# An earlier function table load, small idle products and a new opening order in a memory attention and feed-forward kernel

## The chip, the cores and the metric

The kernel runs on one core of a Trainium2 chip. The time is the device time of one execution in microseconds; of several executions the median counts. A core has the engines TensorE (PE in the profile, its weight loads PEld), VectorE (DVE), ScalarE (ACT), GpSimd (POOL), and queues that issue DMA transfers, here those of SyncE (SP) and ScalarE.

## What is computed

Attention in which the keys and values of a sequence of 576 are first summed into 32 memory slots per head, and a two-layer feed-forward network behind it:

```python
def _attn_ref(q, k, v, phi):                    # 8 batches, 8 heads, 576 rows, head size 64
    a = phi - np.max(phi, axis=2, keepdims=True)
    a = np.exp(a)
    a = a / (np.sum(a, axis=2, keepdims=True) + 1e-09)
    k_m = np.einsum('bhsm,bhsd->bhmd', a, k)
    v_m = np.einsum('bhsm,bhsd->bhmd', a, v)
    scores = scale * np.matmul(q, k_m.transpose(0, 1, 3, 2))
    scores = scores - np.max(scores, axis=-1, keepdims=True)
    attn = np.exp(scores)
    attn = attn / (np.sum(attn, axis=-1, keepdims=True) + 1e-09)
    return np.matmul(attn, v_m).astype(np.float32)

def _moe_ref(x, w_in, w_out):                   # 4608 rows, 512 -> 2048 -> 512
    h = x @ w_in
    g = np.maximum(0.01 * h, h)
    return (g @ w_out).astype(np.float32)
```

The weights arrive as 64-bit floats, and the kernel turns their bits into 32-bit floats itself.

## The kernel before

The kernel is written as small steps, each a Python function under a short name in the table `steps`. Three strings list the names in the order in which the steps are issued: OPENING (line 39), LATER (line 70), and both are run once, one after the other, under a manual schedule (line 1609). Each engine works through its own instructions in that order, and so does each DMA queue; semaphores make an engine wait where it needs another's result. The order is thus written out by hand, and a step stands behind all earlier steps that use its engine.

Names that matter here. `a0.` to `a7.` are the batches' attention, `i0.` to `i3.` and `o0.` to `o3.` the quarters of w_in and w_out, `u0.` to `u7.` the first group of rows (192 rows of each of two blocks) by eighths of the hidden width, `P8`, `V8` and so on the groups behind it, `z.` products that compute nothing that is used.

For batch 0:

- `a0.phi0` to `phi3` load phi by pairs of heads, two of them on ScalarE's queue (`load_phi`, line 542); `k0`.., `v0`.. and `q0`.. load the rest on SP's queue.
- `A10` to `A13` (line 622) take maxima over the rows on VectorE, `A2` (663) transposes them, `A3` (667) makes two diagonal matrices of the maxima, one on VectorE and one on ScalarE (673), and `B0` (679) spreads them to all partitions by products with ones.
- `B10` to `B12` (688) subtract the maximum, `B20` to `B22` (694) are the exponentials on ScalarE, `B30` to `B32` (710 to 719) add them up.
- `C100` to `C102` (738) are the slot sums over k and `C11` those over v: 72 f32 products each of 64 rows by 32 columns, four column places and two row places of TensorE's array. `C2`, `C30`, `C3k`, `C31` divide by the sums.
- `R0` to `R5` (933) transpose q, `Q0` to `Q5` keep it; `D10`, `D3` make the keys' transpose, `D11`, `D5` the values'.
- `E10` to `E13` (979) are the scores, `E20` to `E23` (1030) flip them, and `S01` to `S06` are the first chunk's softmax (maximum, subtraction, exponential on ScalarE at 1065, sum, division, flip).
- `a0.T` (566) is one exponential of a column of ones; its output is overwritten later. ScalarE's first activation makes the compiler put a table load ahead of it on that engine.

For the weights, each quarter comes in three pieces of 768, 768 and 512 columns: `ld` loads one on SP's queue (w_in pieces as several transfers, 381 and 385), `h` and `y` turn the low and the high words (395 and 406 on ScalarE, or 397 on VectorE for `h`), `t` puts them together on VectorE (415). The pieces lie in eight slots in turn, which the parts of q use too, so a load waits until the slot's last reader is done. `b` are the squares' sums for a bound (420).

`f00.1` (1156) folds the values of batch 0 into a quarter of w_in, and `f00.2` (1521) copies the result on ScalarE. `u0.P0` (1248) is a product of the first group with it, `V` the leaky function (1255), `O` the down projection (1335): sixteen halves of six f32 products' passes each. `ci.`, `co.`, `e.` and `e2.` make the scales for the later f16 products.

The idle products of `z.f` are one f32 product of 128 by 128 by 512, those of `z.2` two bf16 products of this size, all into one accumulator that nobody reads (1544).

Of the kernel before, what the change touches and what calls it, by code (L numbers as in the profile page):

```python
# [49 lines left out]
i2.h2 o0.t2 i2.h0 u2.V0 o1.t0 a0.S17 o1.t1 o1.ld2 o2.ld0 i2.y0 i2.y1 o2.ld1 u1.O1 u3.P1 u3.V1 o1.h2  # L50
a0.D4 i2.t0 a1.phi a1.kv0 o2.y0 o1.y2 i2.h1 o2.y1 o2.h1 i2.t1 u2.O0 i2.t2 a1.A1 o1.t2 f02.1 u2.P1
u3.P0 a1.A2 o2.ld2 a1.kv1 o2.h0 u2.V1 f02.2 u3.V0 u4.P0 a1.A3 a1.B0 i2.b o2.h2 o2.t0 a1.kv3 a1.kv2
a1.q1 u3.O0 o2.y2 u4.P1 a1.B10 o2.t1 a1.B20 a1.C10 i1.b o2.t2 a1.B3 u4.V0 o1.b a1.C2 a1.q0 a1.C30
u4.V1 a1.C31 a1.C3k o2.b i3.ld0 a1.C4 a1.Q1 u2.O1 a1.Q0 a0.S18 i3.ld1 a1.D11 a1.D2 a1.D10 a1.D4
a1.D5 a1.D3 u3.O1 i3.h1 i3.ld2 o3.ld2 i3.y0 i3.h0 a1.E1 o0.b i3.y1 o3.ld0 i3.h2 i3.y2 a1.E21 i3.t0
# [131 lines left out]
def kernel(  # L187
# [1349 lines left out]
    def idle_products(n, f32):  # L1537
        if not idle_sums:
            idle_sums.append(ps_o.tile([P, NF, P], F32, name="po"))
# [3 lines left out]
        for _ in range(n):  # L1543
            nc.tensor.matmul(idle_sums[0], by, of, start=True, stop=True)  # L1544
# [97 lines left out]
```

## Time and profile before

| | us |
|---|---|
| median of 3 runs | 653.37 |
| lowest and highest of them | 652.44, 655.95 |
| the profiled execution | 652.1 |
| its span, first to last instruction | 650.0 |

What the profile shows of TensorE in the opening, by stretches of 10 us: busy time with the number of products, and the DMA share:

| from, to us | TensorE busy, products | DMA share |
|---|---|---|
| 0 to 10 | 7.69, 19 | 0.84 |
| 10 to 20 | 9.75, 231 | 1.00 |
| 20 to 30 | 7.71, 210 | 0.86 |
| 30 to 40 | 9.99, 42 | 0.97 |
| 40 to 50 | 10.00, 33 | 1.00 |

In the profile, times are microseconds from the first instruction. A line number names the line of the kernel that issued an instruction; a row of a timeline has its start, its duration, the engine, the line, the operation, what is written from what, the count, and in brackets the idle time ahead of it with what ended that. "issue" is time in which an engine waited for nothing that the profile shows. A row of the chain of waits has a start, a length, and what the end of the kernel waited for at that time.

### The profile page before, as it was taken

How to read it: one execution, taken by the hardware profiler on the slowest of the kernel's cores; microseconds unless marked ns; L12 is line 12 of the kernel's file. 1: busy time of each engine (PE TensorE's matmuls, PEld its weight loads, DVE VectorE, ACT ScalarE, POOL GpSimd, SP SyncE). 2: the span in 40 equal slices, each digit the busy share in tenths (PEclk: the TensorE clock that was granted, in tenths of full speed). 3: DMA queues.
4: the chain of work that ended last, by engine and by line, in shares of the span. 5: the costliest groups of instructions: out<-in, count | busy, mean ns of one | idle time of the engine just before them, and what ended most of it. 6: DMA issues, size and time to landing. Idle time of an engine off the chain costs nothing.

```text
span 650.0 us, 17218 instructions
## 1 busy us (share of the span) xinstructions
PE 636.9 (98%) x7305; PEld 482.5 (74%) x7305; DVE 511.0 (79%) x856; ACT 394.2 (61%) x682; POOL 29.9 (5%) x41
## 2 busy tenths in 40 slices
...
GB/s 302 342 363 288 321 42 123 10 23 89 195 9 33 133 151 69 125 100 42 31 126 136 3 32 43 20 126 147 33 22 79 22 29 20 16 29 7 33 1 50
DMA packets 85885, 61.17 MB, mean 94 GB/s; under 512 B 62128, under 2 KB 69040, under 8 KB 85808
## 3 DMA queue, kind: packets, MB, share of 16 engines
...
q8 instruction: 57, 0.93, 0.6%
q10 hardware_dynamic: 480, 0.43, 0.2%
q14 instruction: 20, 0.16, 0.1%
...
## 4 chain that ended last, share of the span: by engine, by line
PE 90%; DMA 5%; ACT 3%; DVE 2%; issue 1%; SPq 0%; ACTq 0%; DVEq 0%
PE po L1446 31%; PE ph L1378 22%; PE po L1335 13%; PE ph L1248 7%; PE ph L1446 5%; PE pa L1156 4%; PE pa L738 3%; PE po L1481 1%; DMA arena<-in_phi_dram 1%; DMA arena<-in_moe_w_out_dram 1%; PE pa L963 1%; PE po L1544 1%; DMA arena<-in_moe_w_in_dram 1%; DMA arena<-in_q_dram 1%; ACT wi L1394 1%
## 5 line engine op out<-in xcount | busy, mean ns | idle before, releaser
L1446 PEld LDWEIGHTS <-arena 128*128 128x128 f16 x2184 | 209.7, 98 | 32.6 <-issue 9.5
L1394 ACT ACTIVATE wi<-ph,g_sc 128x256 f32<-128x256 f32 (+1 forms) x224 | 99.0, 464 | 166.2 <-PE ph L1378 160.4
L1378 PE MATMUL ph<-a,w_mem 128*128 128x256 f16 (+3 forms) x1440 | 145.3, 246 | 2.9 <-ACT wi L1394 2.9
L1378 PEld LDWEIGHTS <-w_mem 128*128 128x128 f16 x1440 | 114.6, 98 | 17.0 <-issue 6.3
L1446 PE MATMUL po<-wo,arena 128*128 128x256 f16 x936 | 122.2, 273 | 0.3 <-issue 0.3
L1446 PE MATMUL po<-arena 128*128 128x256 f16 x936 | 122.1, 273 | 0.0
L1335 PE MATMUL po<-wo,arena 128*128 128x512 f16 (+1 forms) x384 | 110.0, 433 | 0.0
L1423 DVE TENSOR_TENSOR arena<-arena 128x1024 f16<-128x1024 f32 x52 | 63.5, 1222 | 22.4 <-ACT arena L1419 22.4
L1423 DVE TENSOR_TENSOR arena<-wi,arena 128x768 f16<-128x768 f32 (+1 forms) x60 | 54.6, 911 | 10.1 <-ACT arena L1419 10.1
L1415 DVE TENSOR_TENSOR arena<-wi 128x256 f32<-128x256 f32 x104 | 40.4, 430 | 26.2 <-ACT wi L1394 25.7
L1419 ACT CAST arena<-arena 128x1024 f16<-128x1024 f32 x52 | 54.4, 1046 | 7.6 <-DVE arena L1415 7.3
L1248 PE MATMUL ph<-a,w_mem 128*128 128x192 f16 (+2 forms) x304 | 52.3, 317 | 0.0
L1335 PEld LDWEIGHTS <-arena 128*128 128x128 f16 x288 | 27.8, 98 | 29.8 <-issue 0.6
L1419 ACT CAST arena<-wi 128x768 f16<-128x768 f32 (+1 forms) x60 | 46.5, 776 | 1.6
L1415 DVE TENSOR_TENSOR arena<-wi,arena 128x256 f32<-128x256 f32 x104 | 45.7, 439 | 1.8
L1446 PE MATMUL ph<-wo,arena 128*128 128x256 f16 x312 | 42.6, 273 | 0.0
L1121 POOL TENSOR_TENSOR a<-t,a 128x128 f16<-128x128 f32 (+3 forms) x17 | 21.7, 1297 | 442.4 <-ACT a L1116 442.4
L1335 PEld LDWEIGHTS po<-wo,arena 128*128 128x128 f32 x96 | 17.8, 190 | 20.9 <-issue 17.9
L1156 PE MATMUL pa<-wi,vT 64*32 64x512 f16 (+1 forms) x704 | 29.4, 420 | 0.0
L1255 ACT ACTIVATE arena<-ph,g_sc 128x384 f32<-128x384 f32 x32 | 18.5, 580 | 15.8 <-PE ph L1248 15.5
L1248 PEld LDWEIGHTS <-w_mem 128*128 128x128 f16 x240 | 20.6, 98 | 9.7 <-issue 3.6
L1189 ACT ACTIVATE w_mem<-pa 128x512 f16<-128x512 f32 x40 | 22.7, 596 | 8.5 <-PE pa L1156 7.4
...
## 6 DMA issues: line engine op xcount, KB each, us to landing
...
arena<-in_moe_w_out_dram SPq DMA_DIRECT2D x8, 768.0 KB, 8.3
...
```

Of the source, the lines that this page charges most:

```text
L738: nc.tensor.matmul(var["pk"][g][hh * M:(hh + 1) * M, cs], ld["phi"][rows, hh, j, :], ld["kv", hh][rows, kinds[0]:kinds[-1] + 1, j, :], sta ...
L1121: nc.gpsimd.tensor_tensor(piece(lo, tb), piece(t2, tb), piece(hi, tb), ALU.subtract)
L1156: nc.tensor.matmul(pf[g][cols, :], lhs, rhs, start=(n == 0), stop=(n == len(passes) - 1), tile_position=(g * D, hh * M),)
L1189: nc.scalar.activation(tiles(halves(w16(b, j), g)[:, 0]), w(g), AF.Copy, scale=ws)
L1248: nc.tensor.matmul(ph[:, t0:t0 + n * SB], lhs, rhs, start=(m == 0), stop=(m == len(seq) - 1))
L1335: nc.tensor.matmul(po, lhs, rhs, start=(f == 0 and m == 0), stop=(f == NQ * NF - 1 and m == len(seq) - 1),)
L1378: nc.tensor.matmul(ph[:, t0:t0 + n], lhs, rhs, start=(m == 0), stop=(m == len(seq) - 1))
L1394: nc.scalar.activation(dst, ph, AF.Prelu, scale=g_sc2[:, j:j + 1], alpha=SLOPE)
L1415: nc.vector.tensor_tensor(gt[:, x], y, z, op)
L1419: nc.scalar.copy(dst[:, 0], src)
L1423: nc.vector.tensor_tensor(dst[:, 1], src, dst[:, 0], ALU.subtract)
L1446: nc.tensor.matmul(acc, g[:, x, s, u], rhs, start=(h == 0 and j == 0 and u == 0 and m == 0), stop=(j == NQ - 1 and u == 1 and m == 2), ski ...
```

## The change

The diff changes the two strings with the order and adds one kind of step.

- `a0.T` stands right behind the four loads of phi; before, it stood behind `A3` and `B0`.
- A new step `z.t` makes eight f32 products of 64 rows by 32 columns with 64 moving columns, on ones, in the four column places of the array in turn; it stands seven times at the head. The f32 idle products at the head are gone. In all the opening has seven `z.t`, three `z.2`, two `z.1` and four `z.f`, where it had ten `z.2` and six `z.f`.
- The rest of the opening has a new order: `i0.ld0` behind the last load of v, the largest part of phi (`B12`, `B22`) ahead of the others, `C11` ahead of `S02`, `o0.h0` ahead of `f00.2`, `o0.ld1` right behind `o0.ld0`, `u1.P0` ahead of `u0.P0`, `W11.p` and the loads of batch 2 earlier, `e2.` later, and more of this kind.
- From `P8.0` on LATER is the same but for the steps that have moved across the joint of the two strings.

```diff
 OPENING = """
-z.f z.f z.2 a0.phi1 a0.A11 a0.phi2 a0.phi0 a0.phi3 a0.A10 a0.A13 z.f a0.A12 a0.k1 a0.k2 a0.k0 a0.A2
-a0.k3 a0.q3 a0.q1 z.2 z.2 a0.A3 a0.B0 z.f a0.q0 a0.B10 a0.B11 a0.T a0.B20 a0.B21 a0.q2 z.2 a0.B12
-a0.C100 i0.ld1 a0.v3 a0.v1 a0.B22 a0.B30 a0.C101 a0.B31 i0.ld0 a0.C102 a0.R3 a0.B32 a0.C2 a0.Q3
-a0.C30 a0.C3k a0.R1 a0.v0 a0.Q1 a0.R0 a0.D10 a0.v2 a0.D3 a0.R2 a0.Q2 i0.y1 i0.h1 a0.Q0 a0.E10 a0.E11
-i0.ld2 a0.q4 z.2 z.2 z.2 z.2 z.f a0.E21 z.f a0.C11 a0.E20 a0.q5 a0.S01 i0.h0 a0.S02 i0.t1 a0.S03
-o0.ld0 i0.y0 a0.C31 z.2 z.2 i0.h2 i0.y2 a0.D11 a0.S04 i0.t0 a0.R5 a0.R4 a0.D5 i0.t2 a0.S05 i1.ld0
-o0.ld1 i1.ld2 a0.Q5 a0.Q4 a0.S06 f00.1 a0.E12 f00.2 i1.ld1 a0.E13 u0.P0 i0.b a0.C4 a0.E23 a0.E22
...
+a0.phi1 a0.phi2 a0.phi0 a0.phi3 a0.T z.t z.t z.t z.t z.t z.t z.t z.2 a0.A11 a0.A10 a0.A12 a0.A13 a0.A2
+a0.A3 z.1 a0.k3 a0.k0 a0.k1 a0.B0 a0.B12 a0.B10 a0.k2 z.2 a0.B22 a0.B11 z.2 a0.B20 a0.q3 a0.C100
+a0.q0 a0.B30 a0.q1 a0.B21 a0.C101 a0.q2 a0.B31 a0.B32 a0.C102 a0.C2 a0.R3 a0.v3 a0.v0 a0.v1 i0.ld1
+a0.Q3 a0.C30 a0.R1 a0.R0 a0.Q1 a0.v2 a0.C3k a0.D10 a0.Q0 a0.R2 a0.D3 a0.Q2 z.1 a0.E11 a0.E10 i0.ld0
+a0.E20 z.f i0.y1 i0.h1 a0.E21 i0.ld2 a0.q4 a0.S01 a0.C11 a0.S02 a0.q5 a0.C31 a0.S03 i0.h0 i0.y0 z.f
+z.f z.f i0.t1 a0.D11 a0.R5 i0.h2 i0.y2 o0.ld0 o0.ld1 a0.D5 a0.S04 i0.t0 i0.t2 a0.Q5 a0.R4 a0.Q4
+a0.S05 o0.h0 f00.1 a0.E12 i1.ld0 f00.2 a0.S06 i1.ld2 i1.ld1 i0.b a0.E13 u1.P0 u1.V0 o0.y0 u0.P0
...
-    def idle_products(n, f32):
+    def idle_tile():
         if not idle_sums:
             idle_sums.append(ps_o.tile([P, NF, P], F32, name="po"))
+        return idle_sums[0]
+
+    def idle_products(n, f32):
...
-            nc.tensor.matmul(idle_sums[0], by, of, start=True, stop=True)
+            nc.tensor.matmul(idle_tile(), by, of, start=True, stop=True)
...
+    def idle_tiles():
+        for x in range(8):
+            rows, cols = slice(0, 64), slice(x % 4 * 32, (x % 4 + 1) * 32)
+            nc.tensor.matmul(
+                idle_tile()[cols, 0, 0:64], ones[rows, cols], ones[rows, 0:64],
+                start=True, stop=True, tile_position=(0, x % 4 * 32),
+            )
+
+    steps["z.t"] = idle_tiles
```

More of the change, by code (lines that the diff above doesn't have):

```diff
@@ L50 @@
[L50 to L55, printed above, removed]
@@ new lines @@
+o0.ld2 i2.ld0 u0.V0 a0.C4 a0.E23 i1.h0 a0.D2 i1.y2 i1.h2 o0.y1 a0.E22 o1.ld0 o0.t0 o0.h1 a0.S11
+i1.t2 i1.y0 o0.t1 i1.t0 i1.h1 u1.P1 u0.P1 u0.V1 a0.S12 i2.ld2 i2.ld1 u1.V1 i1.y1 o0.y2 u0.O0 o0.h2
+i2.y0 i1.t1 o0.t2 o1.ld1 i2.h0 u1.O0 f01.1 o1.y0 a0.S13 i2.h2 f01.2 o1.ld2 i2.y1 u0.O1 u3.P0 i2.y2
+o2.ld1 a0.S14 o1.h0 o1.y1 i2.t0 i2.h1 a0.S15 o2.ld0 u3.V0 o1.h1 o2.h1 i2.t1 u2.P0 a1.phi i2.t2 u2.V0
+o1.t0 o2.ld2 o1.t1 a1.kv1 o1.h2 a1.kv0 f02.1 a1.kv2 u3.P1 u1.O1 o1.y2 u3.V1 f02.2 a1.A1 u2.O0 o1.t2
@@ new lines @@
+o2.h0 o2.y1 o2.h2 o2.y0 a1.A2 a1.A3 u4.P0 i2.b a0.D4 o2.t1 a1.B0 a1.B10 u2.P1 a1.B20 i1.b o2.y2
+u3.O0 a1.kv3 a1.q0 u2.V1 a0.S16 o2.t0 a1.q1 u4.V0 a1.C10 a1.B3 a1.C2 i3.ld1 u4.P1 o0.b a0.S17 u2.O1
+a1.C30 o2.t2 a1.C31 a1.C3k a1.C4 a1.Q0 a1.D11 u5.P0 a1.D10 a1.D2 o2.b i3.y1 u4.V1 a0.S18 i3.ld0
+i3.ld2 a1.D5 u5.V0 u3.O1 a1.D3 i3.y0 a1.Q1 i3.h1 a1.D4 i3.h0 i3.t1 i3.y2 a1.E1 o3.ld0 o3.ld2 o1.b
+i3.t0 a1.E20 o3.ld1 u4.O0 u5.P1 i3.h2 i3.t2 a1.E22 f03.1 i3.b o3.y2 o3.y0 o3.h0 f03.2 o3.h2 a1.E21
+ci.1 u5.O0 a1.S11 ci.2 a1.S01 a1.S12 a1.S02 a1.S03 w1.1 o3.y1 a1.S13 u5.V1 o3.t0 o3.t2 a1.S04 ci.3
@@ L61 @@
+o3.h1 u6.P0 u6.V0 ci.4 u4.O1 e. a1.S05 o0.s0 u7.P0 u7.P1 o3.t1 a2.kv0 w0.2 w1.2 o3.b W11.p co.1
+a1.S14 co.2 W01.h0 u7.V0 W01.l0 a2.phi a1.S06 u6.O0 u7.V1 i0.k1 a1.S07 W01.h1 co.3 u6.P1 a1.S15 co.4
+o0.s1 a2.A1 u7.O0 a1.S08 o0.k0 u6.V1
 """
@@ L76 @@
-o3.s3 V11.1 P12.0 o1.m1 O10.0 C11 V12.0 o1.n1 L11 P12.1 o1.s2 O10.1 o1.m2 W03.l1 o1.s3 V12.1 W03.l0
-a2.A3 o1.n2 o2.k0 C12 W13.p o2.k2 o2.l0 W13.h1 P13.0 W13.h0 W13.l1 P13.1 W13.l0 V13.0 o2.k1 L12
-V13.1 O11.0 o1.m3 P14.0 o2.l1 V14.0 C13 o2.s0 P14.1 L13 o2.m0 O11.1 a2.B10 V14.1 o1.n3 o2.n0 o2.s1
-P15.0 a2.B20 C14 o2.m1 O12.0 o2.s2 V15.0 o2.n1 o2.m2 a2.C10 L14 P15.1 o2.s3 a2.B3 O12.1 o2.l2 a2.q0
-V15.1 o2.n2 o3.s0 a2.q1 o3.k1 o3.k0 o3.l1 P16.0 P16.1 o3.k2 O13.0 V16.0 C15 o2.m3 o3.s1 O13.1 V16.1
```

44 lines of the change are left out of this document (21 added, 23 removed).

## The prediction

> **What bounds the kernel now.** First the page, for who is busy over the whole span.
>
> ```profile
> span 650.0 us, 17218 instructions
> PE 636.9 (98%) x7305; PEld 482.5 (74%) x7305; DVE 511.0 (79%) x856; ACT 394.2 (61%) x682; POOL 29.9 (5%) x41
> q8 instruction: 57, 0.93, 0.6%
> ```
>
> TensorE is busy for 98% of the span, so time can come only from stretches in which it works on nothing useful. The stage table (start and end, its length, busy time and count of TensorE products, of its weight loads, of VectorE, ScalarE and GpSimd, then granted clock, DMA share and GB/s) splits the span at the first product of the first group's up projection (28.4) and at the first f16 product of the second group (104.4).
>
> ```profile
> 0.00:21.25 21.25, 18.68 (x347) 9.69 (x347) 12.23 (x25) 9.48 (x16) 1.04 (x11) 1.00 0.93 325
> 21.25:23.31 2.06, 0.01 (x2) 0.01 (x1) 1.34 (x4) 0.00 (x0) 0.00 (x0) 1.00 1.01 400
> ...
> 28.40:104.40 76.00, 75.42 (x502) 35.56 (x503) 59.01 (x112) 65.61 (x102) 11.38 (x13) 1.00 0.69 239
> 104.40:650.00 545.60, 537.91 (x6378) 434.26 (x6374) 435.51 (x713) 315.26 (x556) 17.44 (x17) 1.00 0.26 62
> 139.10:141.30 2.20, 2.20 (x141) 1.99 (x144) 2.20 (x4) 0.28 (x1) 0.00 (x0) 1.00 0.00 0
> ...
> 0.00:28.40 28.40, 12.17 (x32) 4.49 (x32) 1.00 0.89 316
> ```
>
> The last row counts L1544, the idle products, alone: 12.17 us of the first 28.4. From 28.4 to 104.4 TensorE idles 0.6 us of 76. The 7.7 idle us of the third stage lie in code whose order the change leaves as it is. So the change is worth what it moves **the first L1248 product, at 28.36**, as far as nothing between there and 104.4 takes it back. The chain of work gives the path to it.
>
> ```profile
> 0.73 3.06 DMA wi<-in_phi_dram
> ...
> 8.32 0.41 ACT r1k L673
> 8.77 0.43 PE pa L679 x2
> ...
> 16.34 3.55 PE po L1544 x12
> 19.89 1.37 PE po L738 x88
> 21.25 2.06 issue
> 23.31 0.42 PE po L738 x22
> ...
> 25.68 1.15 PE pa L1156 x14
> ...
> 27.93 0.43 PE pa L979 x16
> 28.36 2.78 PE ph L1248 x8
> ...
> 90.53 12.87 PE po L1335 x30
> ```
>
> Two places on it are waste. At 21.25 TensorE stops for 2.06 us in the middle of the sums over v (step C11, L738) with nothing to wait for ("issue"). And the timelines of ScalarE and VectorE show the table load behind the maximum, and what else stands still:
>
> ```profile
> 0.73 0.92 ACTq L547 DMA_DIRECT2D wi<-in_phi_dram  x2
> ...
> 7.02 1.28 ACT L673 ACT_TABLE_LOAD   x1 [7.02 <-DVE mx L670]
> ...
> 17.91 0.92 ACT L395 ACTIVATE arena<-arena 128x768 uint32<-128x768 uint16 x1 [0.87 <-DMA arena<-in_moe_w_in_dram]
> 19.46 0.85 ACT L1065 ACTIVATE t<-t 128x768 f32<-128x768 f32 x1 [0.64 <-DVE t L1060]
> 23.79 0.52 ACT L810 ACTIVATE x_v<-po,r 128x64 f32<-128x64 f32 x2 [2.63 <-PE po L738]
> 24.20 0.68 ACT L395 ACTIVATE arena<-arena 128x512 uint32<-128x512 uint16 x1
> 25.47 0.69 DVE L415 SCALAR_TENSOR_TENSOR wi<-arena 128x512 uint32<-128x512 uint32 x1 [2.81 <-ACT arena L406]
> ```
>
> The stop at 21.25 is everybody's: ScalarE idles 2.63 us for C11, and VectorE 2.81 us for ScalarE.
>
> **Part 1, the table load.** Step T moves to behind the two phi issues on ScalarE's queue, done at 1.65; the load ends near 3.0, under the transfer of phi, which holds the first maximum until 3.8. L673 then starts at 7.02 and the second L679 pair follows 1.3 us earlier. What is late next are the exponentials on ScalarE and the adds behind them on VectorE, which keep their length; the new order of their three parts puts the largest first and gives the three k sums (C10) little more than 0.7 of the 1.3 us. What hides the load is the transfer; if that cover were gone, 1.28 us would come back.
>
> **Part 2, where instructions come in.** 57 instruction packets carry 0.93 MB: 16 KB each. TensorE's 7305 loads and 7305 products are 256 for each of the 57, so I take a packet for a block of 256 of its instructions. The stop stands behind 347 + 347 = 694 of them; block edges then lie, by the same count, at 182, 438, 694 and 950. An f32 product is two loads and two products (C11's 72 are 144 products and 144 loads in L738). Idle work before: 32 products with their loads, 64 instructions. After: seven z.t of 8 f32 products are 224, three z.2, two z.1 and four z.f another 32: 256, so +192. Behind the hole stand 22 products and their loads, so it lay 244 instructions into C11's 288, and C11 began at 450; now it begins at 450 - 56 + 244 = 638 (idle instructions ahead of it, old and new). The edges fall now: 182 inside the z.t, 438 early in C102, 694 at 56 instructions into C11, 950 in R4 just ahead of the fold f00.1. **The edges move; they don't leave the fast code.**
>
> Why no hole elsewhere: 144 such products run from 139.1 to 141.3 without one, where the DMA share is 0.00; at 21.25 it is full. I take it that a block is asked for when the edge before it is passed, and waits behind loads. Old: edge 438 lay in the idle products after 16.34, so the block took 5.9 to 7 us until 23.31. New: I put the edges near 4, 11, 17 and 22 us (below), 7, 6 and 5 us apart: no hole at the first, 0 to 1 us in C11, 0 to 2 us ahead of f00.1. The Trainium skill, "Runtime: NRT & Kernel Launch", Instruction fetch mechanics, also has blocks of 256, but gives TensorE room for 2048 instructions and calls the cost of crossing an edge mostly hidden. By that, no stop could stand at 694 and shifting edges would be worth 0; the row at 21.25 speaks against it.
>
> **Part 3, the new order.** Bytes come in the order of SP's queue. SP's issue rows and the tile answers:
>
> ```profile
> 11.81 0.66 SPq L385 DMA_DIRECT2D arena<-in_moe_w_in_dram  x1
> 14.84 1.28 SPq L381 DMA_DIRECT2D arena<-in_moe_w_out_dram  x1
> 25.71 1.28 SPq L385 DMA_DIRECT2D arena<-in_moe_w_in_dram  x3
> L558 SPq DMA_DIRECT2D wo<-in_v_dram x3: 327/607/652, 8.9 to 11.1; - x3
> ...
> DMA to landing us min/median/max: 5.9/7.0/8.2
> ...
> DMA to landing us min/median/max: 4.2/6.9/8.8
> ...
> arena<-in_moe_w_out_dram SPq DMA_DIRECT2D x4, 768.0 KB, 8.8
> ```
>
> (The landing rows are of in_v_dram, then of in_moe_w_in_dram; the last is the median of the first four pieces of w_out.) The last v was issued at 11.1 and landed near 11.1 + 8.2 = 19.3; C11 began near 19.8. In the new order i0.ld0 (768 KB) comes behind it: at the 325 to 400 GB/s of the windows that is 2 to 2.4 us, so v is whole at 17 and C11 runs from 17.4 or so to 19.2 (1.37 + 0.42), against 23.73: 4.5 us earlier, less a hole of 0 to 1.
>
> The next limit is the weight piece i0.ld2, issued at 11.8 and landed near 20.6 in both orders: two conversions of 0.68 on ScalarE and 0.69 on VectorE make 22.7 at the least; ScalarE's own queue (the exponential 0.85, i0.h0 and i0.y0 about 0.92 each, the latter behind i0.ld0 near 19.3) makes it 24. The fold f00.1 ends near 24.3 (27.3 before), or 25.3 if its edge costs a whole us. Its copies f00.2 now stand behind o0.h0 on ScalarE, an added wait: o0.ld0 lands near 14.84 + 8.8 = 23.6 and takes 0.9 (a row of 768 words), so f00.2 runs from 24.6 at the earliest. Queued behind are i0's squares and u1.V0, whom u1.O0 alone needs, some 8 us later. First L1248: 25.2 to 26.8, I take 25.9, against 28.36: **2.5 us**.
>
> SP's wait until 25.71 is for the slot that the q transposes R4 and R5 (L933) free; they come 2 to 3 us earlier, and the DMA hole behind it closes, so later weights keep pace.
>
> **Part 4, behind it.** From the first L1248 to 104.4 the two orders hold the same products. The ends: 0.6 us of idle time can go, and data may be late. ScalarE idles 76.00 - 65.61 = 10.4 us there and five of the sixteen down halves stand at the end of both orders as a reserve, so I take back 0.3. Later edges lie 64 instructions further on, in the fast L738 of later batches too: 0.5 either way, taken as 0.
>
> **The clock.** The first idle f32 products start 0.85 apart, later ones 0.42:
>
> ```profile
> 2.01 0.34 PEld L1544 LDWEIGHTS po<-ones 128*128 128x128 f32 x1 [0.52 <-issue]
> 2.86 0.34 PEld L1544 LDWEIGHTS po<-ones 128*128 128x128 f32 x1 [0.52 <-issue]
> 3.71 0.15 PEld L1544 LDWEIGHTS <-ones 128*128 128x128 bf16 x1 [0.52 <-issue]
> ...
> 6.31 0.30 PE L663 MATMUL pa<-ident,r1k 128*128 128x128 f32 x1 [0.39 <-DVE r1k L622]
> ...
> 18.44 0.19 PEld L1544 LDWEIGHTS po<-ones 128*128 128x128 f32 x1 [0.24 <-issue]
> 18.86 0.19 PEld L1544 LDWEIGHTS po<-ones 128*128 128x128 f32 x1 [0.24 <-issue]
> ```
>
> So TensorE starts at half speed, though the clock column prints 1.00, and has done so from 0.99 until after 3.71 at least. A z.t has the form of the 16 products at 27.93, 0.43 us at full speed: seven are 3.0, or 6.0 at half, from 0.99 to 4 to 7. A2 (L663) is due at 6.3. If the gate opens as before they end by 5.8 and cost nothing; if not, 0.7. The Trainium skill, "TensorE: Matmul & The Clock Gate", Part 1, says that some 3.4 us of activity open the gate, whatever the number of products: the slow starts up to 3.71 here agree. By it the z.t serve as well. But they fill 2 of 4 row groups and 1 of 4 column groups at a time, and no row here shows whether that counts.
>
> **Sum.** -2.5 + 0.3 = -2.2 us (ends -4.0 and +0.5) on the profiled execution's 652.1 (span 650.0): 649.9. The median, 653.37, is 1.3 above it, which gives 651.2. I forecast the middle, **650.6**.
>
> **Rivals.** (A) More comes off: ScalarE reaches f00.2 at 24.6, no edge costs, and the 0.6 us go too: 3.2 + 0.6 = 3.8, 649.0. For it: i0.ld2 and o0.ld0 allow it. Against: three edges in fast code under full DMA. 0.22. (B) The hole only moves, or ScalarE with 65.61 of 76 us becomes the bound ahead of 104.4: 2 us return, gain -0.8 to 1.2, 652.5. For it: edge 950 right ahead of f00.1. 0.16. By the skill's page on the runtime, no edge costs, and only parts 1 and 3 count: about 2 us, inside the forecast. (C) Slower: the small z.t don't open the gate, and it stays shut until the dense L1248. On the chain from 8.77 to 28.36 lie B0, C10 and C11 (0.43, and 1.8 for each 144 products, by 1.37 + 0.42), f00.1 (1.15, and 0.42 taken for its end), 5.6 us at full speed, and E1 and a dozen transposes that I put at 3; half speed doubles them, and the waits for v and i0 cover 2 to 3. Price 6.5 less the gain of 2.5: +4, 657. It decides if the gate is still shut when C10 starts near 10. For it: their small area. Against: C10 and C11 are dense themselves and may open it by 14, which leaves a price near the gain. 0.07. The forecast (gain 1.2 to 3.2) has 0.55.
>
> A measurement tells 0.5% (3.3 us) from no change. Faster by that is A's better part and little more, 0.23; slower is C and a bad B, 0.08; within, 0.69. The range, 648.0 to 654.0, holds A to B with the 1.3 us between profile and median; C stays out.
>
> **What would show it.** Table load before 3.1 and L673 at 7.0. C11 from about 17, done by 20. "issue" stops of under 1 us in L738, or one ahead of L1156. First L1248 at 25.2 to 26.8. TensorE's idle time from there to the second group still under 1 us, and that group's first L1248 in f16 near 102. Wrong would be: idle f32 products 0.85 apart after 6 us (the gate), or TensorE waits for ScalarE among the L1335.

## The result and the profile after

The changed kernel takes 658.48 us (median of 6 runs, 657.56 to 658.91) against 653.05 for the kernel before (6 runs, 651.99 to 655.95): a ratio of 1.0076, 95% interval 1.0054 to 1.0097. It is **slower by 0.8%**, where 650.6 and no loss beyond 654.0 were forecast. The profiled execution took 658.91.

First a correction. The text on the change, its excerpt of the diff and the prediction have seven `z.t`; the kernel that ran has six. So the change adds 160 idle instructions of TensorE, not 192, and each edge lies 32 instructions further on in the program than the prediction put it. The prediction also counted weight loads and products alone. With the semaphore and drain instructions that the trace has in TensorE's queue counted too, the edges (the ends of the blocks of 256) lie behind 193, 449, 705 and 961 instructions, and so on. In loads and products alone, the two stops below lie behind 442 and 694, where the prediction had 438 and 694.

The page of the changed kernel: span, TensorE, instruction packets.

```profile
span 656.8 us, 17385 instructions
PE 637.0 (97%) x7385; PEld 484.9 (74%) x7385; DVE 512.7 (78%) x856; ACT 393.1 (60%) x682; POOL 30.0 (5%) x41
q8 instruction: 58, 0.95, 0.6%
```

TensorE is busy as long as before (636.9) in a span that is 6.8 us longer: the loss shows as idle time of TensorE. The stage table, split at the same events (first L1248, first f16 product of the second group), in the columns that the prediction names:

```profile
0.00:33.48 33.48, 23.87 (x511) 14.85 (x511) 16.76 (x33) 13.55 (x27) 1.04 (x11) 0.90 0.75 272
33.48:109.98 76.50, 75.29 (x507) 35.73 (x502) 60.44 (x112) 64.33 (x102) 11.52 (x13) 1.00 0.67 234
109.98:656.80 546.82, 537.84 (x6375) 434.36 (x6373) 435.50 (x713) 315.18 (x556) 17.44 (x17) 1.00 0.26 63
```

The opening is 5.1 us longer (33.48 against 28.36), the second stage 0.5 (76.50 against 76.00), the third 1.2 (546.82 against 545.60). The chain of waits (start, length, what was waited for) shows where the 5.1 went:

```profile
9.95 1.69 PE po L738 x89
11.63 4.63 issue
16.27 0.68 PE po L738 x31
16.95 0.52 PE po L756 x2
17.46 2.21 PE ph L933 x9
...
21.17 1.00 PE pa L979 x32
22.16 1.06 PE po L1547 x2
23.22 0.62 PE po L738 x43
23.84 1.58 issue
25.42 1.21 PE po L738 x74
...
30.41 0.33 SPq L385
```

**The stop has doubled and moved forward.** Before, TensorE stood once for 2.06 us, in C11. Now it stands for 4.63 us in C10, the sums over k, and again for 1.58 us in C11. Nothing that the profile shows is waited for at either place; a block of instructions is missing. The DMA view from 13.9 to 16.0 us has the packet that ends the first stop (packets, MB, share):

```profile
q8 instruction: 1, 0.02, 3.3%
```

It runs from 13.91 to 15.02, is the first such packet behind the start of the span, and TensorE goes on 1.25 us behind its end. This holds throughout: in the 17 profiles of this document TensorE has 45 stops of over 0.3 us marked "issue". Every one lies at an edge by this count, that is, behind 193 and a multiple of 256, and ends 1.2 to 1.5 us behind the end of an instruction packet. That is what shows that the stops are waits for instructions.

ScalarE's timeline shows the step that worked, and who pays:

```profile
1.67 1.28 ACT L566 ACT_TABLE_LOAD   x1 [1.67 <-PEq L1639]
2.97 0.20 ACT L566 ACTIVATE sq<-ones 128x1 f32<-128x1 f32 x1
6.99 0.40 ACT L673 ACTIVATE r1k<-ident,mx 128x128 f32<-128x128 f32 x1 [3.82 <-DVE mx L670]
...
18.24 0.48 ACT L944 COPY wi<-ph 128x384 f32<-128x384 f32 x1 [8.00 <-PE ph L933]
```

The table is loaded by 2.95 and L673 starts at 6.99, as forecast; C10 starts at 9.88 instead of 10.62. Then ScalarE idles 8.00 us for a transpose that stands behind the stop. The stop also shuts the clock gate, that is, the granted clock falls to half. By stretches of 5 us (length, then per engine; the last three columns are granted clock, DMA share, GB/s):

```profile
10.00:15.00 5.00, 1.64 (x113) 1.47 (x113) 1.78 (x6) 0.24 (x1) 0.00 (x0) 0.92 1.04 390
15.00:20.00 5.00, 3.73 (x45) 3.23 (x46) 1.17 (x4) 1.01 (x3) 0.00 (x0) 0.50 1.05 391
20.00:25.00 5.00, 3.84 (x83) 1.90 (x81) 2.99 (x5) 2.48 (x4) 0.00 (x0) 0.90 0.87 346
25.00:30.00 5.00, 4.58 (x114) 3.01 (x115) 3.04 (x6) 3.36 (x7) 0.00 (x0) 1.00 0.05 16
```

The granted clock is 0.50 from 14.22 to 21.05, so the rest of C10 and the transposes behind the stop run at half speed (E1 starts at 21.10, when the gate is open again). The last row shows the other consequence: the DMA engines stand idle from 25 to 30, because SyncE waits until 30.41 (25.71 before) for the slot that the late q transposes free. Behind the opening the table of TensorE's waits (total us, times, longest) has a row of stops that was not there, the second of these (the first holds the two stops above):

```profile
PE po L738 <- issue: 6.2, 2, 4.6
...
PE pa L738 <- issue: 1.6, 1, 1.6
```

It is a stop at 324.6 in the slot sums of batch 5. A wait of 0.7 us for ScalarE at L1004, in batch 1, is new as well.

### The profile page after: what moved, and what is told of

It is laid out like the page before. It is cut to its first block, busy times and chain, and to the rows that moved or that the text cites. A ratio compares the mean times of both kernels' runs of the same rounds, so it can differ in the third digit from the quotient of the medians.

```text
span 656.8 us, 17385 instructions
## 1 busy us (share of the span) xinstructions
PE 637.0 (97%) x7385; PEld 484.9 (74%) x7385; DVE 512.7 (78%) x856; ACT 393.1 (60%) x682; POOL 30.0 (5%) x41
## 3 DMA queue, kind: packets, MB, share of 16 engines
q1 hardware_dynamic: 85328, 59.64, 32.4%
## 4 chain that ended last, share of the span: by engine, by line
PE 89%; DMA 4%; DVE 2%; ACT 2%; issue 2%; SPq 0%; ACTq 0%; DVEq 0%
PE po L1446 31%; PE ph L1378 22%; PE po L1335 13%; PE ph L1248 6%; PE ph L1446 5%; PE pa L1156 4%; PE pa L738 3%; DMA arena<-in_moe_w_in_dram 2%; DMA arena<-in_phi_dram 1%; PE po L1481 1%; PE pa L963 1%; PE po L1547 1%; DVE r1k L622 1%; ACT wi L1394 1%; PE po L738 1%
## 5 line engine op out<-in xcount | busy, mean ns | idle before, releaser
L1415 DVE TENSOR_TENSOR arena<-wi 128x256 f32<-128x256 f32 x104 | 40.4, 429 | 26.8 <-ACT wi L1394 26.3
L1248 PE MATMUL ph<-a,w_mem 128*128 128x192 f16 (+2 forms) x304 | 52.4, 317 | 0.0
L1335 PEld LDWEIGHTS <-arena 128*128 128x128 f16 x288 | 27.8, 98 | 29.8 <-issue 0.6
L1255 ACT ACTIVATE arena<-ph,g_sc 128x384 f32<-128x384 f32 x32 | 18.5, 581 | 15.6 <-PE ph L1248 15.3
L1248 PEld LDWEIGHTS <-w_mem 128*128 128x128 f16 x240 | 20.7, 98 | 9.4 <-issue 3.3
```

The lines of the kernel that those rows point to most:

```text
L1248: nc.tensor.matmul(ph[:, t0:t0 + n * SB], lhs, rhs, start=(m == 0), stop=(m == len(seq) - 1))
L1335: nc.tensor.matmul(po, lhs, rhs, start=(f == 0 and m == 0), stop=(f == NQ * NF - 1 and m == len(seq) - 1),)
L1415: nc.vector.tensor_tensor(gt[:, x], y, z, op)
```

## The experiments

Two theories at first. **H**: an edge of 256 instructions lies where its block cannot come in time, TensorE stands, and the stop shuts the gate. **R**: the new order of loads and of ScalarE's work costs the time by itself, and the stop only fills a wait that would be there anyway.

What the traces show, for all runs in one table (read from each profiled execution; us). "First packet" is the start of the first instruction packet, "stop" the longest "issue" wait of the place, "half" the time at half clock once the gate has opened, which it does by 6.2 us where the table says nothing else.

| kernel | first packet | stop in C10 | stop elsewhere before the first L1248 | half | first L1248 | span | ratio to before |
|---|---|---|---|---|---|---|---|
| before | 14.76 | none | 2.1, C11 | none | 28.3 | 650.0 | 1 |
| after | 13.91 | 4.6 | 1.6, C11 | opens at 10.8; 14.2 to 21.1 | 33.5 | 656.8 | 1.0076 |
| e1 | 14.23 | none | 4.8, C11 | 22.1 to 28.9 | 32.4 | 653.8 | 1.0011 |
| e2 | 8.93 | none | 2.4, f00.1 | 26.6 to 33.5 | 28.1 | 653.5 | 1.0031 |
| e3 | 14.15 | none | 2.5, C11 | none | 27.7 | 650.8 | 0.9986 |
| e4 | 13.91 | 4.9 | none | 15.3 to 22.1 | 32.1 | 654.6 | 1.0014 |
| e5 | 13.75 | 4.2 | 1.4, C11 | opens at 11.4; 14.8 to 21.6 | 33.3 | 656.5 | 1.0056 |
| e6 | 9.48 | 0.7 | 0.6, C11 | none | 26.8 | 651.6 | 1.0005 |
| e7 | 14.08 | none | 3.6, C11 | 23.1 to 26.5 | 31.2 | 654.9 | one run |
| e8 | 13.77 | 4.1 | 1.4, C11 | opens at 11.7; 15.1 to 21.9 | 33.4 | 656.2 | 1.0072 |
| e9 | 12.50 | 2.9 | none | 16.3 to 19.7 | 29.8 | 653.7 | 0.9990 |
| e10 | 12.17 | 2.4 | 1.1, C11 | opens at 20.6 | 31.7 | 654.4 | 1.0029 |
| e11 | 11.64 | 2.1 | 0.5, C11 | opens at 20.3 | 32.3 | 654.1 | one run |
| e12 | 13.56 | none | 2.8, C11 | opens at 13.3; 23.5 to 26.9 | 30.6 | 655.5 | 1.0039 |
| e13 | 11.72 | 2.6 | 1.9, C11 | 8.5 to 18.8 | 31.7 | 654.9 | 1.0033 |
| e14 | 13.33 | none | 3.0, C11 | 21.7 to 28.6 | 30.0 | 653.3 | 0.9989 |
| e15 | 14.05 | 3.3 | none | opens at 13.9; 17.3 to 20.7 | 31.6 | 653.8 | 0.9994 |

### The parts of the change, e1 to e4

e1 is the changed kernel with the idle head of before:

```diff
-a0.phi1 a0.phi2 a0.phi0 a0.phi3 a0.T z.t z.t z.t z.t z.t z.t z.2 a0.A11 a0.A10 a0.A12 a0.A13 a0.A2
+a0.phi1 a0.phi2 a0.phi0 a0.phi3 a0.T z.f z.f z.2 a0.A11 a0.A10 a0.A12 a0.A13 a0.A2
```

> The changed kernel with the old head: z.f z.f z.2 in place of the six z.t and z.2. Theory H (instruction packets that come late behind the loads, and the clock gate that the holes and the small products leave shut): the gate opens near 4.4 us as before, the block edges move by 184 instructions, so that C10 holds one edge early in it and C11 holds two, 256 instructions apart; no stop in C10, first L979 near 14.5, a stop of 3 to 6 us near the end of C11; first L1248 at 28 to 30, time 651 to 655. Rival R (the new order of the loads and of ScalarE's work is what costs): the head makes no difference, first L1248 stays near 33.5, time 657 to 659.

654.87 us (653.24 to 655.9), ratio 1.0011 (0.9997 to 1.0025). C10 runs from 9.59 through, but two edges now fall into C11, and the second stops it for 4.8 us, 8 products before its end. The first L1248 comes at 32.4, where H had 28 to 30. By windows:

```profile
18.10:22.10 4.00, 0.22 (x24) 0.06 (x6) 1.63 (x2) 0.00 (x0) 0.00 (x0) 1.00 1.06 406
22.10:23.10 1.00, 0.01 (x3) 0.02 (x3) 0.00 (x0) 0.00 (x0) 0.00 (x0) 0.50 0.96 389
23.10:28.90 5.80, 5.80 (x15) 2.42 (x16) 3.74 (x6) 3.95 (x7) 0.00 (x0) 0.50 0.30 117
```

The gate shuts 3.8 us into the stop and the three z.f behind it take 5.5 us at half clock. The stop left C10 with the head, so it belongs to the edges (H), but the new order alone gained nothing.

e2 is the kernel before with the new head:

```diff
-z.f z.f z.2 a0.phi1 a0.A11 a0.phi2 a0.phi0 a0.phi3 a0.A10 a0.A13 z.f a0.A12 a0.k1 a0.k2 a0.k0 a0.A2
+z.t z.t z.t z.t z.t z.t z.2 a0.phi1 a0.A11 a0.phi2 a0.phi0 a0.phi3 a0.A10 a0.A13 z.f a0.A12 a0.k1 a0.k2 a0.k0 a0.A2
```

> The kernel before with the new head: six z.t and z.2 in place of z.f z.f z.2, everything else in the old order, the table load too. Theory H: the gate doesn't open before 9 us, a stop of 3 to 5 us in C10 near the place of the changed kernel's, first L1248 at 31 to 34, time 656 to 660. Rival R: as before within 1 us, 652 to 654.

656.5 us (654.44 to 659.38), ratio 1.0031 (1.0007 to 1.0054). The head costs in the old order too, but not in the way that H had it: only the time is as expected. The gate opened at 6.15 (H: not before 9), the first packet came early, at 8.93, C10 and C11 had no stop, and the first L1248 came at 28.1 (H: 31 to 34). The stop now lay ahead of f00.1, and the gate shut behind it, under the dense L1248:

```profile
25.00:26.60 1.60, 0.90 (x18) 0.41 (x21) 1.25 (x4) 0.00 (x0) 0.00 (x0) 1.00 0.88 305
26.60:33.40 6.80, 6.80 (x49) 3.88 (x38) 1.55 (x4) 4.25 (x6) 0.83 (x1) 0.50 0.99 365
```

e3 is the kernel before with T alone moved behind phi:

```diff
-z.f z.f z.2 a0.phi1 a0.A11 a0.phi2 a0.phi0 a0.phi3 a0.A10 a0.A13 z.f a0.A12 a0.k1 a0.k2 a0.k0 a0.A2
-a0.k3 a0.q3 a0.q1 z.2 z.2 a0.A3 a0.B0 z.f a0.q0 a0.B10 a0.B11 a0.T a0.B20 a0.B21 a0.q2 z.2 a0.B12
+z.f z.f z.2 a0.phi1 a0.A11 a0.phi2 a0.phi0 a0.phi3 a0.T a0.A10 a0.A13 z.f a0.A12 a0.k1 a0.k2 a0.k0 a0.A2
+a0.k3 a0.q3 a0.q1 z.2 z.2 a0.A3 a0.B0 z.f a0.q0 a0.B10 a0.B11 a0.B20 a0.B21 a0.q2 z.2 a0.B12
```

> The kernel before with T alone moved to behind the issues of phi. Both theories: the load runs from 1.7 to 3.0, L673 at 7.0, C10 starts 0.7 us earlier. H: the stop in C11 moves little, since its packet sets its end; first L1248 0 to 0.7 us earlier, time 652 to 653. If the chain to C10 carries through to the end: 1.3 us less, 651.7.

653.08 us (651.12 to 655.74), ratio 0.9986 (0.9966 to 1.0007). C10 starts 1.4 us earlier, at 9.21, the first L1248 0.6 earlier; the stop in C11 is 2.5 us. Later TensorE waits 1.8 us for ScalarE at L480 and 0.6 at L498, which are not among the longest waits of before.

e4 is the changed kernel with the f32 products of the old head ahead of the six z.t, to open the gate without moving the edges by more than four instructions:

```diff
-a0.phi1 a0.phi2 a0.phi0 a0.phi3 a0.T z.t z.t z.t z.t z.t z.t z.2 a0.A11 a0.A10 a0.A12 a0.A13 a0.A2
+a0.phi1 a0.phi2 a0.phi0 a0.phi3 a0.T z.f z.f z.t z.t z.t z.t z.t z.t a0.A11 a0.A10 a0.A12 a0.A13 a0.A2
```

> The changed kernel with z.f z.f ahead of its six z.t (z.2 left out): the gate open as before, the edges within 8 instructions of the changed kernel's. It parts the gate from the packets. H: gate open near 4.4, z.t end near 7.3, so A2 is about 1 us late; a stop in C10 remains, 2 to 5 us, but TensorE's work behind it is at full speed unless the stop shuts the gate again; first L1248 at 29 to 32.5, time 654 to 657.5. If the shut gate alone were the cause: no stop, first L1248 near 27, time 650 to 652.

656.43 us (650.97 to 658.18), ratio 1.0014 (0.9989 to 1.0040). The gate opens at 5.0 instead of 10.8, and the profiled run still stops in C10:

```profile
PE po L738 <- issue: 4.9, 1, 4.9
```

So a late gate is not what starves C10. R falls too: e1, e4 and the changed kernel have the same order and ratios of 1.0011, 1.0014 and 1.0076. What differs in their profiles is where the edge lies, when its packet comes, and the gate.

### The loads and the place of the edge, e5 to e7

e5 and e6 put `i0.ld1` ahead of the three v loads, as before had it; e5 in the changed kernel, e6 in e4's:

```diff
-a0.q0 a0.B30 a0.q1 a0.B21 a0.C101 a0.q2 a0.B31 a0.B32 a0.C102 a0.C2 a0.R3 a0.v3 a0.v0 a0.v1 i0.ld1
+a0.q0 a0.B30 a0.q1 a0.B21 a0.C101 a0.q2 a0.B31 a0.B32 a0.C102 a0.C2 a0.R3 i0.ld1 a0.v3 a0.v0 a0.v1
```

> The changed kernel with the 512 KB load i0.ld1 issued ahead of the three v loads, as the kernel before has it (a0.v3 a0.v0 a0.v1 then follow it); everything else is the changed kernel. The first instruction packet landed at 13.9 us in the changed kernel and in e4, and at 8.9 us in e2, which differ in the order of the loads. If the order of the loads sets when the packet comes through (theory L), the packet lands well before 11.6 us, the 4.6 us hole in C10 goes, the gate stays open after 10.8, and the first L1248 starts near 28 to 29 us instead of 33.5: 652 to 654.5 us. If it is not the order of these loads but how many of them have been issued by then, or something else about the new opening (theory N), the packet still lands near 13.9 us, the hole stays at 11.6 to 16.3, and the time is 657.5 to 659 us.

> e4's head (two 128x512 f32 idle products ahead of six small ones) with z.2 dropped, and i0.ld1 ahead of the three v loads as in e5. The gate should open near 5.0 us as in e4. Theory L: no hole in C10, the first L1248 near 26 us, and 650 to 652.5 us, below the kernel before. Theory N: the hole of 4.9 us at 11.2 stays, gate shut for 6.8 us after it, 655.5 to 657 us as in e4.

e5: 658.63 us, ratio 1.0056 (1.0035 to 1.0077), packet at 13.75, stop of 4.2: as the changed kernel. e6: 654.17 us, ratio 1.0005 (0.9978 to 1.0031), packet at 9.48, stop of 0.7 in C10, gate open throughout. The order of the loads is not the cause, as e5 shows; e6's early packet is **chance**: e15 below has the same instructions as e6 up to 40 us, and its packet came at 14.05. Six of e6's ten runs have a mean granted clock of 0.999 or 1.000 and take 652.2 to 654.4 us; four have 0.991 to 0.995, which is the shut gate, and take 656.5 to 657.9. e4 splits in the same way, four at 651.0 to 654.5 and six at 656.3 to 658.2. The means of the two groups differ by 4.1 us in e6 and 4.0 in e4. That this is the price of the late packet, stop and shut gate together, is inferred: one run of each was profiled, e6's a fast one with an early packet, e4's a slow one with a late packet.

e6 also shows that the order was not the gain that it seemed:

```profile
0.00:26.78 26.78, 22.21 (x512) 12.88 (x512) 16.88 (x33) 13.50 (x27) 1.05 (x11) 1.00 0.94 336
26.78:104.90 78.12, 75.65 (x508) 35.82 (x502) 60.59 (x112) 64.53 (x102) 11.85 (x13) 1.00 0.66 230
104.90:651.60 546.70, 537.85 (x6375) 434.40 (x6373) 435.45 (x713) 315.48 (x556) 17.43 (x17) 1.00 0.26 63
```

The first L1248 comes at 26.78, where the prediction had 25.2 to 26.8; the two stages behind it then take 2.1 and 1.1 us more than before (76.00 and 545.60). e15 takes that up.

e7 is the changed kernel with 48 idle instructions at the head instead of 196, so with edges elsewhere again:

```diff
-a0.phi1 a0.phi2 a0.phi0 a0.phi3 a0.T z.t z.t z.t z.t z.t z.t z.2 a0.A11 a0.A10 a0.A12 a0.A13 a0.A2
+a0.phi1 a0.phi2 a0.phi0 a0.phi3 a0.T z.f z.f z.t z.2 z.2 a0.A11 a0.A10 a0.A12 a0.A13 a0.A2
```

> The changed kernel with the head z.f z.f z.t z.2 z.2: 120 idle instructions where the changed kernel has 224 and e1 has 88 there. If blocks of 256 instructions set the place of the holes, the first edge moves into the first half of C10, the second between C10 and C11 and the third to some 180 instructions into C11: no hole within C10, one of 2 to 5 us within C11 or just ahead of it. If the hole belongs to C10 itself (its data or its buffers), it stays at 113 products into C10.

657.03 us in one run. (The expectation counts too many: up to C11 there are 64 idle instructions here, 212 in the changed kernel and 28 in e1; the third edge lies some 236 instructions into C11.) No stop in C10, 0.8 us in E1 (L979), 3.6 us in C11, where it was expected: the stop follows the edge, not the step.

### Why the first packet is late, e8 to e13

Theory D: it stands in line behind the loads. To hold the loads back, one element of a tile that is loaded later is written by VectorE first, and SyncE waits for that. e8 holds q and all behind it until A3:

```diff
                 nc.vector.tensor_scalar_mul(diag[:, 0, :], ident, mx2[:, 0:1])
+                if b == 0:
+                    ld["q", 1] = ld_slot()[:, 0:2 * KJ * D].rearrange(
+                        "p (hh j d) -> p hh j d", hh=2, j=KJ
+                    )
+                    nc.vector.tensor_copy(ld["q", 1][:, 1, 0, 0:1], mx2[:, 0:1])
```

> The changed kernel, with one element of the first q tile written by VectorE right after A3 (L672, near 7.3 us): SyncE waits for it with the first q load, and with every load behind it, so that only phi and k are in transfer until then. k should land near 7.3 us and the DMA engines lie quiet from there to near 9 us. Theory D (the instruction packet waits because the DMA engines are full): the first packet, asked for near 3.0 us, comes in when k is through, at 7 to 9 us instead of 13.9, and C10 runs without the 4.6 us hole. Theory N (the packet's time is set by something in the program near C10, about 3.5 us after it starts): it still starts at 13.5 to 14 us, with a hole of 2.5 us or more within C10. The time itself says little, since q comes some 4 us later.

659.28 us, ratio 1.0072 (1.0046 to 1.0098). The DMA share falls to 0.28 from 7 to 8 us and 0.49 from 8 to 9, and the packet comes at 13.77 all the same, with a stop of 4.1.

e9 and e10 hold v and all behind it until B11, e9 in e4's kernel with the four v loads in a row, e10 in the changed kernel:

```diff
-            steps[f"{name}B1{i}"] = lambda js=js: sub_max(js)
+            def less_max(i=i, js=js):
+                sub_max(js)
+                if b == 0 and i == 1:
+                    nc.vector.tensor_copy(ld["kv", 3][:, 1, 0, 0:1], var["mx"][:, 0, 0:1])
+            steps[f"{name}B1{i}"] = less_max
```

> The changed kernel with e4's head (two 128x512 f32 idle products ahead of six small ones, z.2 dropped), the four v loads in a row right behind q, i0.ld1 behind them, and one element of the first v tile written by VectorE behind B11 (near 9.7 us): SyncE holds v and all that follows until then, so that the DMA engines run dry when q has landed near 10.3 us. Theory D: the first packet comes in by 10.4 us in every run, no hole over 1 us in C10, none over 1 us in C11, the gate open from 5.0 us on, first L1248 near 26 us: 651 to 653 us and no runs near 657. Theory N: the hole of 4.9 us stays in part of the runs, as in e4 and e6 (0.994 to 0.995 mean clock, 656 to 658 us).

> The changed kernel with that one element alone: VectorE writes it into the first v tile behind B11, so that v and the loads behind it are held until near 9.7 us; head and order as changed. Theory D: the first packet by 10.4 us, no hole in C10 (under 1 us), the gate opens near 11 us and does not shut again, first L1248 near 28 us, C11 later by up to 3 us as v2 lands later: 653 to 655 us. Theory N: hole of 4.6 us at 11.6, 658 to 660 us.

e9: 654.46 us, ratio 0.9990 (0.9964 to 1.0017). e10: 656.57 us, ratio 1.0029 (1.0009 to 1.0049). The packets come at 12.50 and 12.17, some 1.5 us earlier than in the changed kernel, and the stops are 2.9 and 2.4 us. But the engines moved nothing from 10 to 11 us in e9, and the packet did not come then. Neither D nor its rival N (the stop and the packet as without the quiet) fits.

e11 makes the quiet longer: q and all behind it wait for B11.

```diff
-            steps[f"{name}B1{i}"] = lambda js=js: sub_max(js)
+            def less_max(i=i, js=js):
+                sub_max(js)
+                if b == 0 and i == 1:
+                    ld["q", 1] = ld_slot()[:, 0:2 * KJ * D].rearrange(
+                        "p (hh j d) -> p hh j d", hh=2, j=KJ
+                    )
+                    nc.vector.tensor_copy(ld["q", 1][:, 1, 0, 0:1], var["mx"][:, 0, 0:1])
+            steps[f"{name}B1{i}"] = less_max
```

> The changed kernel, with one element of the first q tile written by VectorE behind B11 (near 9.7 us), so that q and every load behind it are held until then: phi and k alone are in transfer, and the DMA engines should lie quiet from about 8.5 to 11.5 us. In e8 to e10 the first packet came at 12.2 to 13.8 us although the engines had been nearly idle for a microsecond before. Theory Q (the request of the first idle products stands in a queue and gets through once the engines are free): packet at 8.5 to 9.5 us, no hole in C10. Theory E (the request is not made at the block's first edge, near 3 us, but only when PE has come to the end of its block, near 11.4 us, or shortly before): packet at 12.1 to 12.8 us, about 1 us behind PE's reaching the end, hole of 2.5 to 3 us in C10. The time itself says little, as q comes 7 us later.

656.23 us in one run. Windows of 1 us, then TensorE's timeline (L745 is L738 in this kernel):

```profile
7.00:8.00 1.00, 0.75 (x5) 0.42 (x6) 0.20 (x1) 0.30 (x1) 0.00 (x0) 1.00 0.25 95
8.00:9.00 1.00, 1.00 (x4) 0.40 (x4) 0.92 (x2) 0.20 (x1) 0.00 (x0) 1.00 0.00 0
9.00:10.00 1.00, 1.00 (x10) 0.21 (x9) 0.86 (x4) 1.00 (x3) 0.00 (x0) 1.00 0.00 0
10.00:11.00 1.00, 1.00 (x76) 1.00 (x74) 0.85 (x4) 0.15 (x1) 0.00 (x0) 1.00 0.35 57
```

```profile
11.51 0.35 PE L745 MATMUL po<-wi,wi 64*32 64x64 f32 x2
13.99 0.34 PE L745 MATMUL po<-wo,wi 64*32 64x64 f32 x6 [2.13 <-issue]
```

For two whole microseconds the DMA engines move nothing, and the packet of the edge that was crossed at 3.5 us does not come. It starts at 11.64, when TensorE has just run out, and TensorE goes on at 13.99. So **the packet was not in the queue behind the loads since its edge**. That full engines make it later once it is asked for (11.64 here, 13.91 in the changed kernel) is likely, but each figure is from one profile.

e12 is e9 with two z.t instead of six, which puts the first edge into C10, in the quiet:

```diff
-a0.phi1 a0.phi2 a0.phi0 a0.phi3 a0.T z.f z.f z.t z.t z.t z.t z.t z.t a0.A11 a0.A10 a0.A12 a0.A13 a0.A2
+a0.phi1 a0.phi2 a0.phi0 a0.phi3 a0.T z.f z.f z.t z.t a0.A11 a0.A10 a0.A12 a0.A13 a0.A2
```

> e9 with two small idle steps instead of six: 128 fewer instructions, which moves the edges by half a block: the first into C10 (near 10.4 us, asked for while the DMA engines are quiet), the second into the products between C10 and C11, the third to some 216 instructions into C11. If a request made inside C10 is served within about 1 to 2 us when the engines are quiet, there is no hole over 1 us behind C10 and one of 0 to 2 us in C11, the gate stays open, and the first L1248 starts near 27 us in all runs: 652 to 653.5 us. If packets need 3.4 us or more also there, PE stands 1 to 2 us behind C10 and 3 to 4 us in C11 as in e7: 655 to 657 us.

656.33 us, ratio 1.0039 (1.0022 to 1.0056). From the edge at 11.34 the packet needs 2.2 us; no stop in C10 or behind it, but 2.8 us in C11, and the gate shuts. The packet came nearly as fast as the first alternative had it, the time is the second's.

e13 is the changed kernel with the head of before and the six z.t between B0 and C10, so that the first edge is crossed near 9 us and the second stays in C10:

```diff
-a0.phi1 a0.phi2 a0.phi0 a0.phi3 a0.T z.t z.t z.t z.t z.t z.t z.2 a0.A11 a0.A10 a0.A12 a0.A13 a0.A2
-a0.A3 z.1 a0.k3 a0.k0 a0.k1 a0.B0 a0.B12 a0.B10 a0.k2 z.2 a0.B22 a0.B11 z.2 a0.B20 a0.q3 a0.C100
+a0.phi1 a0.phi2 a0.phi0 a0.phi3 a0.T z.f z.f z.2 a0.A11 a0.A10 a0.A12 a0.A13 a0.A2
+a0.A3 z.1 a0.k3 a0.k0 a0.k1 a0.B0 a0.B12 a0.B10 a0.k2 z.t z.t z.t a0.B22 a0.B11 z.t z.t z.t a0.B20 a0.q3 a0.C100
```

> The changed kernel with the head of before (z.f z.f z.2) and the six small idle steps put between B0 and C10 in place of two z.2, so that the first edge is crossed near 8 to 9 us instead of near 3 us, while the second stays some 226 instructions into C10. If the packet is asked for at the edge and takes 3.4 us (theory P), it starts near 12 us, and PE stands 1.5 to 2.5 us in C10; the gate opens near 5.0 us and does not shut. If an early edge gives nothing because the packet comes at a point of the program tied to C10 itself (theory C), it starts near 13.9 us again, with a hole of 4 to 4.6 us and a shut gate behind it, 656 to 659 us.

656.64 us, ratio 1.0033 (1.0015 to 1.0051). The packet starts at 11.72, 2.7 us behind its edge at 9.05 and 2.2 us **earlier** than in the changed kernel, whose edge is crossed 5.6 us earlier. The stop in C10 is 2.6 us, as theory P had it. What P had wrong is the gate. Windows of e13:

```profile
5.00:8.50 3.50, 2.25 (x68) 1.28 (x70) 2.27 (x6) 0.40 (x1) 0.00 (x0) 1.00 1.02 372
8.50:9.40 0.90, 0.90 (x51) 0.90 (x40) 0.76 (x2) 0.90 (x3) 0.00 (x0) 0.52 1.07 401
9.40:11.30 1.90, 1.90 (x125) 1.89 (x117) 1.64 (x5) 0.45 (x2) 0.00 (x0) 0.50 1.05 399
```

The gate shuts at 8.54 with TensorE at work on the z.t since 7.67. In e1, with z.2 in this place and the same head, it stays open until 22.1, although TensorE is busy for no longer in the same stretch:

```profile
5.00:8.50 3.50, 2.09 (x12) 0.74 (x10) 2.28 (x6) 0.40 (x1) 0.00 (x0) 1.00 1.02 370
```

Why an early edge brings no early packet stays **open**. The traces leave three facts: with the first edge crossed in C10 or just ahead of it (9 to 11.4 us), the packet starts 2.2 to 4.2 us later; with the edge crossed among the head's idle products at 3.5 to 7.1 us it starts at 8.9 to 14.1, with the same opening at times early and at times late (e6, e15); and it is not the queue of loads that holds it (e11).

One reading is left that no run tests. Behind an edge in the head, the next instructions wait for the maxima; behind one in C10 they run at once. Counted not from the edge but from the 20th instruction behind it, the packet starts 1.7 to 6.2 us later in all 17 profiles, against 2.2 to 10.5 from the edge. So the block may be asked for some instructions behind the edge. That would be only part of the answer: e4 and e6 reach this place at 7.76 and 7.73, and their packets start at 13.91 and 9.48.

### What is left of the gain, e14 and e15

e14 runs e3's kernel again, in more rounds.

> e3's kernel once more, in more rounds: the order and the head of before with the table load alone moved behind phi. It was the only kernel so far below the kernel before, at a ratio of 0.9986 with an interval from 0.9966 to 1.0007. If the 0.7 us that C10 gains outlasts the batch (theory T), the ratio is 0.9975 to 0.9992 and its interval ends below 1; if the gain is used up by the waits of 1.8 and 0.6 us at L480 and L498 (theory W), it is 0.9995 to 1.001.

653.06 us (652.1 to 655.86, 12 runs), ratio 0.9989 (0.9974 to 1.0004). Twice 0.1% below before, twice not told from no change. Its profiled run has the waits at L480 (1.0 us) and L498 (0.6) again, and a stop of 3.0 us in C11.

e15 adds 96 idle instructions to e6 near 40 us, which brings all later edges back to where before had them (e6 has 164 idle instructions more than before, and 164 + 96 is 4 more than 256):

```diff
-i2.y0 i1.t1 o0.t2 o1.ld1 i2.h0 u1.O0 f01.1 o1.y0 a0.S13 i2.h2 f01.2 o1.ld2 i2.y1 u0.O1 u3.P0 i2.y2
+i2.y0 i1.t1 o0.t2 o1.ld1 i2.h0 u1.O0 z.s f01.1 o1.y0 a0.S13 i2.h2 f01.2 o1.ld2 i2.y1 u0.O1 u3.P0 i2.y2
...
+    def late_tiles():
+        t = ps_a.tile([P, D], F32, name="pa")
+        for x in range(24):
+            rows, cols = slice(0, 64), slice(x % 4 * 32, (x % 4 + 1) * 32)
+            nc.tensor.matmul(
+                t[cols], ones[rows, cols], ones[rows, 0:64],
+                start=True, stop=True, tile_position=(0, x % 4 * 32),
+            )
+
+    steps["z.s"] = late_tiles
```

> e6's kernel with 96 more idle instructions (24 small products into an accumulator of their own, ahead of f01.1 near 40 us), so that the edges behind them lie within six instructions of where they lay in the kernel before. In e6 the first L1248 comes 1.5 us earlier than before, but its profile has two further holes that before has not, 1.5 us in the C10 of batch 1 (61.6) and 1.4 us in that of batch 5 (320.9). If those come from the edges alone (theory M), both are under 0.5 us here, the 96 instructions cost 0.9 us, and the time is 1.5 to 2 us below e6's: 650 to 651 us in runs without a hole in batch 0's C10, a median of 651 to 653 us, ratio 0.995 to 0.9985. If they come from something else in the new order (theory O), they stay, and the time is 0.9 us above e6's, 654 to 655.5 us.

653.2 us (650.88 to 657.73, 12 runs), ratio 0.9994 (0.9969 to 1.0020): not below before as a whole. By the mean granted clock it has two kinds of runs: eight in which the gate does not shut again take 650.9 to 654.9, with a median of 651.66 (653.18 for e6's six); four in which it does take 656.0 to 657.7. The profiled run is one of the four, but its later stages answer whether the stops stay. TensorE's waits of e6, then of e15:

```profile
PE pa L738 <- issue: 2.9, 2, 1.5
PE po L738 <- issue: 1.3, 2, 0.7
```

```profile
PE po L738 <- issue: 3.3, 1, 3.3
...
PE po L1446 <- issue: 0.7, 1, 0.7
```

Both stops of batches 1 and 5 (pa) are gone, as theory M had it: they went with the edges. What they cost in time is not settled by the runs. The median of those in which the gate does not shut again is 1.5 us below e6's although 96 instructions were added, but the means differ by 0.9 us (652.29 against 653.21), and the kernel before was 0.8 us faster beside e15 than beside e6 (653.76 against 654.58). No version here is faster than before beyond what the measurement tells.

## Why the prediction was wrong, point by point

- **Part 1, the table load**: right. Loaded by 2.95, L673 at 6.99, C10 0.74 us earlier (forecast: little more than 0.7). Alone it measures 0.9986 and 0.9989 (e3, e14).
- **Part 2, the blocks**: right that blocks of 256 set the stops, that the edges move, and roughly where they fall (the forecast had PE pass them near 11 and 17 us). The miscount of one z.t put the second edge too early, but still in C10. **The step that failed** is "no hole at the first". It took a block to be asked for when the edge before it is passed and to need 5.9 to 7 us. The first edge was passed at 3.5 us, and TensorE could go on behind the second only at 16.27: 12.8 us. The 5.9 to 7 came from one stop of the kernel before, whose earlier edge was passed at 17.36 among idle products that ran without a break; the first edge of the new head is followed by waits for the maxima. e2, e4, e6, e11 and e13 show that the time from the first edge to its packet is no fixed cost (2.7 to 8.2 us in these, 10.5 in the changed kernel) and partly chance. Why, stays open. The term was 0 and measured 4.63.
- **Part 2, C11**: forecast 0 to 1 us, measured 1.58.
- **Part 3, the order**: the first L1248 was forecast at 25.2 to 26.8 and came at 33.48. e6, with nearly no stop, has it at 26.78, so the loads and ScalarE's queue were judged about right. SP's wait, which was to end 2 to 3 us earlier, ended at 30.41 instead of 25.71, because the slot's readers stand behind the stop; in e6 it ends at 23.71, as forecast.
- **Part 4, later edges**: "0.5 either way, taken as 0". They lay 96 instructions further on, not 64. Measured: a stop of 1.57 us in batch 5 in the changed kernel, and 2.9 us in two stops in e6, most of the 3.2 us by which e6's later stages are longer and more than the 1.5 us that it had gained in the opening. e15's profile shows that they go with the edges. The mechanism was named, but its size was not bounded by the one stop known, 2.06 us, at each later pass through L738.
- **The clock, rival C**: its result came (657 forecast, 658.48 measured), its first half also: six z.t and a z.2 do not open the gate. It opens at 10.81 in the changed kernel, at 6.15 with one z.f right behind them (e2) and at 5.0 with two z.f ahead of them (e4), though even with these at 13.3 and 13.9 in e12 and e15. These rows show the four z.2 products ahead of C10 in the changed kernel and then in e6, half the speed against full:

```profile
8.06 1.89 PE L1547 MATMUL po<-ones 128*128 128x512 bf16 x4
```

```profile
8.04 1.04 PE L1547 MATMUL po<-ones 128*128 128x512 bf16 x4
```

  But C's price did not come from that. C10's dense products opened the gate at 10.81, and it was the stop that shut it again, which no rival had; that its number came near is luck. By two single profiles with an equally late packet, the closed head costs 2.2 us of span (656.8 against e4's 654.6); the late packet, as inferred above, costs some 4 us.
- **Weighing the page against the row**: the Trainium skill, "Runtime: NRT & Kernel Launch", Instruction fetch mechanics, calls an edge mostly hidden. Stops of 0.5 to 4.9 us at counts of 449, 705 and 961 speak against it here, as the one at 21.25 did.
